# One pass over 512-token chunks for the feed-forward block and its backward, with token-major activations made by DMA transposes

## The chip, the cores and the metric

The kernel runs on one core of one Trainium2 chip. The metric is the device time of one execution in microseconds (us). The engines are named as the profile names them: PE is TensorE (matrix products), DVE is VectorE, ACT is ScalarE, POOL is GpSimd, and SP is SyncE, which issues most DMAs. "PEclk" is the TensorE clock that was granted, as a share of full speed.

## The reference, cut to what matters

A transformer block with modulated layer norms, forward, and then the gradients of all its nine inputs. There are 2048 tokens, D = 512, 32 heads of 16, and F = 1792 hidden features. All is bf16.

```python
h = layernorm(x) * (1 + ca) + sa
x = x + ga * (attention(h @ wqkv) @ wo)
h = layernorm(x) * (1 + cb) + sb          # xn2 is the normalised x, h2 this h
r = relu(h @ w1 + b1);  s = r * r
x = x + gb * (s @ w2 + b2)
# ... then jax.vjp of all this with grad_out
```

The backward of the feed-forward needs the same two large activations in two layouts. With `gf = gb * grad_out`, `ds = gf @ w2.T` and `dz = 2 * r * ds`, the input gradient `dz @ w1.T` wants s and dz *feature-major* (features on the 128 partitions), as does `s @ w2`. The weight gradients `dw1 = h2.T @ dz` and `dw2 = s.T @ gf` contract over tokens, so they want s and dz *token-major*. Each of the two tensors is 2048 x 1792 x 2 bytes, or 7.3 MB. One chunk of 512 tokens has 14 x 4 = 56 blocks of 128 x 128, that is 56 x 32 KB = 1.835 MB.

## The kernel before

The kernel before gets the second layout by computing the product a second time. The phases run one after another over all 2048 tokens, with DRAM in between. P is 128, DC is 4 (blocks of D), FC is 14 (blocks of F), QC is 4 (chunks of 512 tokens), TT is 16 (tiles of 128 tokens).

```python
# dense stage 1, feed-forward (cut)
for qc in range(QC):
    for fc in range(FC):                       # z, feature-major
        for ic in range(DC):
            PE.matmul(pz[:], w1_nat[:, ic, fc*P:(fc+1)*P], h2T[:, ic, qc*512:(qc+1)*512], ...)
        DVE.tensor_scalar(rT[:, fc, :], pz[:], b1col[:, fc:fc+1], 0.0, ALU.add, ALU.max)
    SP.dma_start(out=rT_st[qc], in_=...rT)     # to DRAM, for the backward
    DVE.tensor_tensor(sT[:], rT[:], rT[:], ALU.mult)
    for qi in range(4):
        t = qc*4 + qi
        for (f0, W) in fchunks:                # z AGAIN, token-major
            for ic in range(DC):
                PE.matmul(pzt[:, 0:W], h2T[:, ic, t*P:(t+1)*P], w1_nat[:, ic, f0:f0+W], ...)
            PE.matmul(pzt[:, 0:W], ones_bf[0:1, 0:P], b1row[0:1, f0:f0+W], ...)
            DVE.tensor_single_scalar(rtok[:, f0:f0+W], pzt[:, 0:W], 0.0, ALU.max)
        SP.dma_start(out=rtok_st[:, t, :], in_=rtok[:])
        DVE.tensor_tensor(stok[:], rtok[:], rtok[:], ALU.mult)
        SP.dma_start(out=stok_st[:, t, :], in_=stok[:])
        ...                                    # s @ w2, output
# weights for the backward (cut): w1T, w2T, gfT by DMA transposes, then
for t3 in range(3):
    for hg in range(HG):
        ...                                    # tmpT <- 128 columns of wqkv, transposed
        for hq in range(4):                    # 96 copies of 16 partitions x 1 KB
            SP.dma_start(out=wT_pad[o0:o0+DH, ..., :], in_=tmpT[r0:r0+DH, :])
# dense stage 2: ds, dzT, dz @ w1.T, backward of LN2 (cut)
# dense stage 3 (cut): ds AGAIN, token-major, 256 matmuls
#     DVE: dztok = 2 * ds * rtok (rtok reloaded), stored to dztok_st
# dw1: for each of 4 blocks of D, reload all of dztok (POOL and SP in turn)
# dw2: for each of 2 halves of F, reload all of stok
# then da, dO = da @ wo.T, dwo
# tail, after the backward of attention: dqkv, dh1 = dqkv @ wT_pad, backward of LN1
```

## Time and profile before

The time is 3955.47 us (median of 4 runs, 3953.62 to 3963.21). The table of windows gives, for each stretch of the span, its length and the busy time of each engine. It is the best first view here, because each stage has another limit and the page's shares average over them.

In the view below the columns are: window, its length, then PE, PEld (weight loads), DVE, ACT and POOL busy in us (with instruction counts), PEclk, the mean share of the 16 DMA engines that was busy, and GB/s. These are the windows of the kernel before, from attention forward to attention backward.

```profile
284.00:1223.00 939.00, 867.80 (x4102) 162.44 (x4101) 33.23 (x55) 938.90 (x1025) 19.14 (x31) 0.50 0.05 12
1223.00:1305.00 82.00, 32.95 (x195) 18.13 (x198) 67.53 (x234) 4.46 (x17) 0.61 (x1) 0.65 0.37 130
1305.00:1494.00 189.00, 184.07 (x784) 71.11 (x799) 140.42 (x192) 0.00 (x0) 0.00 (x0) 0.99 0.32 125
1494.00:1618.00 124.00, 11.81 (x27) 3.30 (x29) 10.11 (x24) 0.00 (x0) 6.93 (x1) 0.52 0.40 92
1618.00:1731.00 113.00, 110.99 (x468) 43.92 (x477) 93.05 (x326) 0.00 (x0) 0.00 (x0) 0.97 0.19 67
1731.00:1814.00 83.00, 54.45 (x244) 25.43 (x247) 44.26 (x88) 0.00 (x0) 1.29 (x2) 0.86 0.81 220
1814.00:1990.00 176.00, 103.04 (x251) 34.53 (x256) 11.94 (x30) 7.40 (x16) 17.16 (x32) 0.51 0.62 179
1990.00:2100.00 110.00, 57.47 (x219) 20.50 (x225) 3.12 (x3) 7.15 (x13) 15.28 (x24) 0.90 0.60 181
2100.00:2216.00 116.00, 68.95 (x335) 30.38 (x339) 53.47 (x127) 2.77 (x5) 48.22 (x58) 0.78 0.38 130
2216.00:3660.00 1444.00, 1237.81 (x10221) 343.94 (x10220) 1188.47 (x1024) 1118.68 (x2208) 139.78 (x102) 0.85 1.15 202
```

Row by row these are: attention forward; output projection and LN2; feed-forward forward; weights for the backward; backward product; second dz product; dw1; dw2; dO and dwo; attention backward. Attention forward is ScalarE without a gap (938.90 of 939). Attention backward is busy on PE, VectorE and ScalarE, and the change leaves its instructions as they are. What the change is meant to shorten is the 993 us between: PE is busy for 624 of them and no engine is full. The feed-forward row is PE-bound (184 of 189, clock 0.99); the row after it has 11.81 us of PE in 124 us.

Two views show what these rows hold. First the second products, as groups of the dense stages (line, engine, operation, names, shapes, count, busy us, mean ns of one, idle before): `pzt` is z again (product and its bias row), `pzg` is ds again. Together they are 60.0 + 22.9 + 56.6 = 139.5 us of PE, on top of the copies out of PSUM.

```profile
L433 PE MATMUL pzt<-w_nat,xn2T 128*128 128x512 bf16 (+1 forms) x252 | 60.0, 355 | 0.2
L566 PE MATMUL pzg<-w2T,gfT 128*128 128x512 bf16 (+1 forms) x251 | 56.6, 376 | 25.8 <-DVE dztok L568 25.4 <-issue 0.2
...
L435 PE MATMUL pzt<-b1row,ones_bf 1*128 1x512 bf16 x64 | 22.9, 358 | 0.0
```

Second, the queue of SyncE in the empty row (start, duration, name, count): groups of 16 small copies into `wT_pad` take 10 us each, about 0.63 us apiece, for 75 us in all with the transposes between. The loads for the next stage (`rTb` and `xn2b`) stand behind them, and VectorE waits 79.7 us for the first of these.

```profile
1535.31 10.30 SPq L487 DMA_DIRECT2D wT_pad<-tmpT  x16
...
1611.61 0.35 SPq L510 DMA_DIRECT2D rTb<-rT_st  x1
1612.02 0.89 SPq L528 DMA_DIRECT2D xn2b<-xn_st  x2
```

And the wait of VectorE in the dense stages (who waited, for whom: total us, times, longest). The view names `xn2b`, but the instruction at L518 reads `rTb` and not `xn2b`; the load of `rTb` is the one just ahead of it on the same queue:

```profile
DVE dzT L518 <- DMA xn2b<-xn_st: 79.7, 1, 79.7
```

### The profile page before, as it was taken

The numbers are of one execution on the slowest core, as the hardware profiler recorded it, in microseconds if no ns is written. First come the engines' busy times: TensorE is split into PE (matmuls) and PEld (weight loads), VectorE is DVE, ScalarE is ACT, GpSimd is POOL, SyncE is SP. The second block draws the span as 40 slices with busy tenths as digits, with TensorE's granted clock in tenths as the row PEclk, the third lists the DMA queues.
The fourth block names the chain that finished last, engine by engine and source line by source line (L and its number), as shares of the span: only waits on it lengthen the run. The fifth ranks groups of instructions, "written<-read, shape, count | busy, mean of one in ns | idle before, by whom it ended". The sixth has DMA issues, their size and how long they took to land. (4 is left out here: it accounts for less than half of the span.)

```text
span 3961.6 us, 49677 instructions
## 1 busy us (share of the span) xinstructions
PE 3084.2 (78%) x18427; PEld 898.6 (23%) x18501; DVE 2005.1 (51%) x3136; ACT 2143.6 (54%) x3486; POOL 279.7 (7%) x306
## 2 busy tenths in 40 slices
PE   3689999999996891676655788988888888888656
PEld 1231111111112330232222222222222222222212
DVE  7750000000006771563005587878878787887581
ACT  0019999999993000000000577877777787877211
POOL 2000000000000000000014110101010110101000
PEclk7885555555556895786587788879888887998877
DMA  3130000000002234246654799999999999999213
GB/s 120 63 123 5 15 17 16 17 16 15 6 5 97 111 132 94 99 113 207 180 171 148 157 198 209 203 203 208 203 210 197 212 198 209 196 200 197 105 49 102
DMA packets 1230145, 497.83 MB, mean 126 GB/s; under 512 B 1162051, under 2 KB 1192263, under 8 KB 1228109
## 3 DMA queue, kind: packets, MB, share of 16 engines
q1 hardware_dynamic: 1207246, 464.23, 55.2%
q0 software_dynamic: 6144, 28.32, 2.4%
q10 hardware_dynamic: 16512, 2.10, 0.4%
q8 instruction: 146, 2.39, 0.2%
q14 instruction: 97, 0.79, 0.1%
HBM read 126.45 MB, written 82.47 MB: 53 GB/s over the span
## 5 line engine op out<-in xcount | busy, mean ns | idle before, releaser
L754 DVE TENSOR_TENSOR dS_u<-psD_u,E_u 128x1024 bf16<-128x1024 f32 x1024 | 1188.5, 1216 | 297.2 <-PE psD_u L752 216.8
L742 ACT ACTIVATE E_u<-psS_u 128x512 bf16<-128x512 f32 x1536 | 868.8, 636 | 290.5 <-PE psD_u L752 276.1
L311 ACT ACTIVATE ET<-psST 128x1024 bf16<-128x1024 f32 x1024 | 938.8, 1770 | 0.0
L308 PE MATMUL psST<-qt_sb,kt_sb 32*128 32x512 bf16 x2048 | 622.7, 597 | 79.7 <-DMA kt_sb<-KtP 8.8
L740 PE MATMUL psS_u<-ik,iq 32*128 32x512 bf16 x1536 | 515.1, 429 | 14.1 <-ACT E_u L742 7.3
L326 DVE COPY ostage<-oacc 128x512 f32<-128x512 f32 x32 | 22.1, 692 | 914.3 <-PE oacc L322 828.4
L752 PE MATMUL psD_u<-iv,ido 32*128 32x512 bf16 x2048 | 444.3, 428 | 22.5 <-DVE dS_u L754 16.3
L792 PE MATMUL dqacc<-dsT,KS_tok 128*32 128x512 bf16 x2048 | 212.2, 501 | 161.2 <-DMA dsT<-dS_u 133.3
L742 ACT ACTIVATE E_u<-psS_x 128x512 bf16<-128x512 f32 x512 | 334.9, 654 | 3.7 <-PE psD_u L752 1.9
L322 PE MATMUL oacc<-ET,vaug 128*32 128x512 bf16 x2048 | 316.6, 608 | 0.6 <-ACT ET L311 0.6
L595 ACT ACTIVATE w1blk<-aw_0_12805 128x512 bf16<-128x512 f32 x1 | 0.6, 597 | 556.6 <-PE aw_0_12805 L591 556.6
L308 PEld LDWEIGHTS <-kt_sb 32*128 32x128 bf16 x2048 | 105.3, 99 | 557.6 <-issue 557.6
L777 PE MATMUL accVK<-E_u,dOs_tok 128*16 128x512 bf16 x2048 | 225.3, 430 | 0.0
L740 PE MATMUL psS_x<-ik,iq 32*128 32x512 bf16 x512 | 207.5, 405 | 1.0
L740 PEld LDWEIGHTS <-iq 32*128 32x128 bf16 x2048 | 100.1, 92 | 358.2 <-issue 357.5
L752 PEld LDWEIGHTS <-ido 32*128 32x128 bf16 x2048 | 124.7, 92 | 239.4 <-issue 218.0
L807 POOL TENSOR_TENSOR dQacc<-dQacc,dqtmp 128x512 f32<-128x512 f32 x64 | 81.1, 1268 | 849.9 <-ACT dqtmp L802 849.9
L515 PE MATMUL pds<-gfT,w2T 128*128 128x512 bf16 x219 | 55.2, 404 | 108.3 <-DVE dzT L518 79.0
L768 PE MATMUL accVK<-dS_u,qz_14371 128*32 128x512 bf16 x1024 | 112.0, 427 | 6.1 <-ACT vkb L780 6.1
L768 PE MATMUL accVK<-dS_u,qz_14372 128*32 128x512 bf16 x1024 | 111.5, 424 | 6.2 <-ACT vkb L780 5.9
L264 PE MATMUL ppad<-xn1T,wpadT 128*128 128x512 bf16 x376 | 97.0, 402 | 21.7 <-DVE stagep L267 16.2
L322 PEld LDWEIGHTS <-vaug 128*32 128x32 bf16 x2048 | 56.9, 101 | 224.1 <-issue 224.1
(1253 smaller groups left out, 2864.4 us busy)
## 6 DMA issues: line engine op xcount, KB each, us to landing
dzld<-dztok_st POOLq DMA_DIRECT2D x32, 448.0 KB, 3.7
dzld<-dztok_st SPq DMA_DIRECT2D x32, 448.0 KB, 3.4
dsT<-dS_u SPq DMA_TRANSPOSE x512, 4.8
rT_st<-rT SPq DMA_DIRECT2D x4, 1792.0 KB
rtok_st<-rtok SPq DMA_DIRECT2D x16, 448.0 KB, 2.5
stok_st<-stok SPq DMA_DIRECT2D x16, 448.0 KB
rTb<-rT_st SPq DMA_DIRECT2D x4, 1792.0 KB
rtokb<-rtok_st SPq DMA_DIRECT2D x16, 448.0 KB, 11.4
```

Source lines behind the costliest of these rows:

```text
L264: PE.matmul(pp[:], wpadT[:, ic, which, hg, :], h1T[:, ic, qc * 512:(qc + 1) * 512], start=(ic == 0), stop=(ic == DC - 1))
L308: PE.matmul(ps[:, hi, :], kt_sb[r:r + 32, kt * P:(kt + 1) * P], qt_sb[r:r + 32, qc * 512:(qc + 1) * 512], start=True, stop=True, tile_posi ...
L311: ACT.activation(ET[:, 2 * pair:2 * pair + 2, :], ps[:], AF.Exp, scale=SCALE)
L322: PE.matmul(oacc[32 * hq:32 * hq + 32, :], lhsT, ET[:, hq, :], start=(kt == 0), stop=(kt == TT - 1), tile_position=(0, 32 * hq), skip_grou ...
L740: PE.matmul(psS[:], st["q"][r:r + 32, qt * P:(qt + 1) * P], st["k"][r:r + 32, kc * 512:kc * 512 + 512], start=True, stop=True, tile_positi ...
L742: ACT.activation(bst[u][0][:, hq, :], psS[:], AF.Exp, scale=SCALE)
L752: PE.matmul(psD[:, hi, :], st["do"][r:r + 32, qt * P:(qt + 1) * P], st["v"][r:r + 32, kc * 512:kc * 512 + 512], start=True, stop=True, til ...
L754: DVE.tensor_tensor(dS_u[:, 2 * pair:2 * pair + 2, :], psD[:], E_u[:, 2 * pair:2 * pair + 2, :], ALU.mult)
L768: PE.matmul(cur["vk"][32 * hq:32 * hq + 32, :], hst[hg]["qz"][:, qt, hq, :], bst[u][1][:, hq, :], start=(qt == 0), stop=False, tile_positi ...
L777: PE.matmul(acc[32 * hq:32 * hq + DH, :], dOs_tok[:, qt, (hg * 4 + hq) * DH:(hg * 4 + hq + 1) * DH], E_u[:, hq, :], start=False, stop=(qt ...
L792: PE.matmul(acc[32 * hq:32 * hq + 32, :], KS_tok[:, kc * 4 + kt, h * DH:h * DH + 32], tT[:, :, hq * 4 + kt, :], start=(kt == 0), stop=(kt ...
L807: POOL.tensor_tensor(dst2, dst, tmp[:], ALU.add)
```

## The change

The intent: keep a chunk of 512 tokens on the chip from the output projection through the feed-forward, its backward and dO, and get the token-major s and dz by DMA transposes of the feature-major tiles. That removes the second products, most stores and reloads between the phases, and the stage that waits for weights: the padded transposed projection weight is built by POOL's own DMA queue under attention forward and kept in DRAM until the tail. The weight gradients then become one stage that loads each operand once. Attention forward runs by query chunk instead of by head group. Some elementwise work also moves: half of the relus go to ScalarE, h2 and the output's sum to POOL, and LN2's sums become one instruction. The first lines of the diff below remove; cuts are marked.

```diff
-                for (f0, W) in fchunks:
-                    ...PE.matmul(pzt[:, 0:W], h2T[:, ic, t*P:(t+1)*P], w1_nat[:, ic, f0:f0+W], ...)
-                    DVE.tensor_single_scalar(rtok[:, f0:f0+W], pzt[:, 0:W], 0.0, ALU.max)
-                SP.dma_start(out=rtok_st[:, t, :], in_=rtok[:])
-                ...                                # stok, second dz stage, rT store and reload
+        def dense_chunk(c):                        # called for c = 0..3, one after another
+            SP.dma_start(out=O_c[:], in_=o_st[:, ts, :]);  ...x0_c, g_c
+            SP.dma_start(out=OT..., in_=flat(O_c), transpose=True)
+            ...                                    # gf, gfT (transpose), a = O @ wo, x1, LN2 -> xn2_c
+            SP.dma_start(out=xn2T..., in_=flat(xn2_c), transpose=True)
+            ...                                    # h2T = xn2T * (1 + cb) + sb
+            for fc in range(FC):
+                ...PE.matmul(pz, w1_nat, h2T)      # rT on ACT and DVE in turn, sT = rT * rT on DVE
+            SP.dma_start(out=s_tok[:], in_=flat(sT), transpose=True)      # 56 blocks
+            SP.dma_start(out=stok_st[c], in_=flat(s_tok))
+            ...                                    # f = sT.T @ w2, output
+            for fc in range(FC):
+                ...PE.matmul(pds, w2T, gfT)        # dzT = 2 * ds * rT
+            SP.dma_start(out=dz_tok[:], in_=flat(dzT), transpose=True)    # 56 blocks
+            SP.dma_start(out=dztok_st[c], in_=flat(dz_tok))
+            ...                                    # dz @ w1.T, backward of LN2 -> dx1_c, da_c
+            SP.dma_start(out=daT..., in_=flat(da_c), transpose=True)
+            ...                                    # dO = da @ wo.T, dOT (transpose), to dOtP
-                    SP.dma_start(out=wT_pad[...], in_=tmpT[r0:r0 + DH, :])     # after feed-forward
+                    POOL.dma_start(out=wT_bld[...], in_=tmpT[r0:r0 + DH, :])   # under attention forward
+        POOL.dma_start(out=wT_st[:], in_=wT_bld[:])
+        # one weight-gradient stage: gf, O, da, h2 and all of s and dz loaded once,
+        # 4 + 14 + 4 output blocks of dwo, dw2, dw1
+    SP.dma_start(out=wT_pad[:], in_=wT_st[:])       # first load of the tail, 2 MB
-funits = [(hg, qc, kt) ...]                         # attention forward
+funits = [(qc, hg, kt) ...]
```

## The prediction

> **What bounds the kernel now.** Read as stages from the table of windows: projections 0-284 us; attention forward 284-1223 (ScalarE busy 938.9 of 939: saturated, PE clock 0.50); dense middle 1223-2216; attention backward 2216-3660 (DVE 1188, PE 1238 of 1444, DMA share 1.15); tail 3660-3962. The change acts on the dense middle, 993 us, where no engine is full: PE busy is 624 of 993.
>
> Inside it: output projection and LN2 82 us (PE 33); MLP forward 189 (PE 184, clock 0.99, so PE-bound); weight transposes 124 (PE 12; the DMA queue's timeline shows 96 wT_pad issues of 0.62 us, and behind them DVE waits 79.7 us); backward product 113 (PE 111); second dz product 83; dW1 176 (PE 103, clock 0.51, starved by dzld loads); dW2 110 (PE 57); dO, dwo 116.
>
> **Removed.** The 256+64 matmuls of the token-major s product and the 256 of the second dz (0.23 us each: 480 took 111 us in the backward product): about 125 us of PE. The 124 us stage: wT_pad is built during attention forward, where DMA share is 0.05; w1T, w2T and woT remain (w1T issue 1.26 us each). Four reloads of dz and two of s (44 MB) become one.
>
> **Added.** Per chunk 208 blocks of 128x128 through DMA transposes. The backward attention moves 16 blocks in about 2.8 us under load, landing in 4.8, so 36 us of DMA per chunk; s and dz (56 blocks, estimate 10-12 us each) hide under 13 us of matmuls; O, xn2, dA, dO do not hide.
>
> **The new critical path.** The instruction order runs chunks one after another. Per chunk, estimated from the durations: z 15, f 13, ds 12, dh 19 (VectorE, about 3.5 us per tile), dA transpose 6, dO 9, O load and transpose 10, projection and LN 15, xn2 transpose 5, h2 1: about 104 us, PE idle for some 40 of it. The skill's "TensorE: Matmul & The Clock Gate", Part 1, has 216 ns per warm 512-column matmul and half speed after an idle window; the trace agrees (clock 0.99 in the MLP, 0.53 in LN2).
>
> Chunk 0 waits for weights (queued ahead of its xn2 transpose), about 45 us after attention; four chunks then end about 435 us after attention. The weight-gradient stage reloads 22.7 MB (early loads ran near 330 GB/s: 7 MB in 21 us) against 544 matmuls (118 us): about 155-165 us, the first 21-30 exposed. Dense middle: about 615-640 us instead of 993.
>
> **Elsewhere.** Projections start about 10 us sooner (x before g). Attention forward may stall 0-30 us near its third head load: seven tmpT transposes precede it in the DMA queue, each waiting on eight POOL copies. Attention backward unchanged (same instructions). Tail +8 us (wT_pad, 2 MB, loaded ahead of the first tiles).
>
> **Predicted: 3600 us, range 3530 to 3680; faster 0.96, same 0.03, slower 0.01.**
>
> **What would show it.** No pzt or pzg groups; dense middle near 630 us in four repeats of about 104, PE busy about 60%; waits on xn2, dA and O transposes of about 5 us or more in each chunk; dW stage 150-170 with PE idle at its start on loads; attention forward within 940-970; backward 1440-1450.
>
> **What would make it wrong.** Large transposes far slower than 10-12 us (then dz waits on s's buffer, which sT, dzT and dOp share: +10-20 per chunk); attention forward blocked longer by POOL's copies; PE clock at half in the gappy chunks (+30 per chunk); gradient loads near 200 GB/s (+25).

## The result, and the profile after

The changed kernel takes 3624.12 us (median of 4 runs, 3619.38 to 3629.43) against 3955.47 us. The ratio is 0.916, with a 95% interval of 0.914 to 0.918. A ratio here is the mean time of one kernel's fast runs over the mean of the other's fast runs of the same rounds, so it is not quite the ratio of the medians that are quoted. The time is 24 us above the predicted 3600 and inside the range of 3530 to 3680.

The windows after, with the same columns. The rows are: attention forward; the gap until the first feed-forward product; chunks 0, 1, 2; chunk 3 with the wait for the gradients' loads; weight gradients with the first loads of attention backward.

```profile
290.00:1236.00 946.00, 869.25 (x4102) 163.53 (x4101) 33.42 (x56) 939.11 (x1025) 61.83 (x120) 0.50 0.11 33
1236.00:1301.00 65.00, 6.09 (x19) 2.66 (x21) 12.83 (x32) 3.88 (x6) 8.70 (x3) 0.55 0.81 200
1301.00:1408.00 107.00, 68.57 (x272) 26.48 (x275) 62.20 (x145) 7.41 (x12) 21.37 (x25) 0.79 0.60 150
1408.00:1517.00 109.00, 68.84 (x272) 26.59 (x276) 62.55 (x145) 7.40 (x12) 22.01 (x26) 0.80 0.58 145
1517.00:1626.00 109.00, 69.01 (x271) 26.71 (x276) 62.64 (x145) 7.40 (x12) 21.83 (x26) 0.80 0.59 140
1626.00:1744.00 118.00, 63.43 (x255) 24.84 (x261) 53.19 (x126) 4.81 (x7) 14.21 (x24) 0.76 0.67 161
1744.00:1874.00 130.00, 114.26 (x546) 53.92 (x555) 12.68 (x18) 13.06 (x22) 3.55 (x2) 0.93 0.51 198
```

The dense middle, 993 us before, is now 1236 to 1874, that is 638 us. On the spans of the two profiles (3961.6 and 3621.8 us) the balance is: from attention forward's last product to the first dS of attention backward 997.4 to 639.2 (-358), and elsewhere +18: attention forward starts 6 us later and lasts 6 us longer, the tail (from the last dS, which is VectorE's product in attention backward) is some 9 us longer, and attention backward is some 3 us shorter. A chunk takes 107 to 109 us, of which PE is busy for 69, at a clock of 0.79 to 0.80. So the chunk is a chain, not a wall of product, as predicted. These are PE's waits in chunk 1 (who waited, for whom: total us, times, longest):

```profile
PE pm L441 <- DMA T_10570<-O_m: 16.6, 1, 16.6
PE pm L472 <- DVE h2T L460: 13.7, 1, 13.7
PE prow L407 <- DVE proda L542: 5.4, 2, 2.7
PE pm L557 <- DMA T_10501<-da_c: 4.1, 1, 4.1
```

The transposes of O and dA, LN2 with the transpose of xn2 (the wait for h2T) and LN2's backward (the wait for `proda`) are the gaps: 4.1 + 16.6 + 13.7 + 5.4 us. The transposes of s and dz do not appear among the waits. The wait for O holds dO's transpose too: before chunk 3, dO's issues at 1596.27 us and takes 5.92, and O's comes behind it on the queue, at 1602.29.

Three spots cost more than predicted. At the front of chunk 0, PE waits for the first weights and then for h2T, whose transpose of xn2 stands on the queue behind 37 us of weight transposes. PE's timeline (start, duration, engine, line, operation, names, shapes, count; in brackets the idle time before it and what ended it):

```profile
1256.83 0.59 PE L441 MATMUL pm<-wo_nat,T_9372 128*128 128x512 bf16 x1 [15.03 <-DMA wo_nat<-in_A_wo_dram]
...
1301.53 8.69 PE L472 MATMUL pm<-h2T,w_nat 128*128 128x512 bf16 x32 [39.31 <-DVE h2T L460]
```

SyncE's timeline of the same stretch: w2T, w1T, woT, and only then xn2.

```profile
1259.17 13.69 SPq L399 DMA_TRANSPOSE w2T<-in_B_w_dram  x4
1272.90 18.51 SPq L401 DMA_TRANSPOSE w1T<-in_B_w_dram  x14
1291.46 5.17 SPq L403 DMA_TRANSPOSE woT<-in_A_wo_dram  x4
1296.74 1.93 SPq L457 DMA_TRANSPOSE T_9439<-xn_c  x1
```

In the last chunk the transpose of dA takes four times as long to issue as in the others. This is the view of its line (shortest, median and longest duration in ns, first and last start), chunk 2 first, then chunk 3:

```profile
L547 SPq DMA_TRANSPOSE T_11100<-da_c x1: 3113/3113/3113, 1580.3 to 1580.3; - x1
L547 SPq DMA_TRANSPOSE T_11699<-da_c x1: 12062/12062/12062, 1689.4 to 1689.4; - x1
```

The one thing that comes ahead of it only in chunk 3 is the store of db1. SyncE's timeline:

```profile
1678.81 0.58 SPq L586 DMA_DIRECT2D out_dram<-db1bf  x1
```

At the very start, VectorE casts 512 numbers for 17.69 us. VectorE's timeline, first of the kernel before:

```profile
15.18 4.54 DVE L117 CAST crows<-cbf 1x512 f32<-1x512 bf16 x1 [13.75 <-DMA cbf<-in_c_dram]
```

The same cast in the changed kernel, where its input comes earlier but its end, at 19.7 us, is the same:

```profile
2.02 17.69 DVE L112 CAST crows<-cbf 1x512 f32<-1x512 bf16 x1 [0.60 <-DMA cbf<-in_c_dram]
```

### The profile page after: what moved, and what is told of

The parts are those of the page before. It is cut to its first block, busy times and chain, and to the rows that moved or that the text cites. A ratio compares the mean times of both kernels' runs of the same rounds, so it can differ in the third digit from the quotient of the medians.

```text
span 3621.8 us, 47309 instructions
## 1 busy us (share of the span) xinstructions
PE 2861.2 (79%) x17554; PEld 811.5 (22%) x17605; DVE 1861.7 (51%) x2725; ACT 2166.0 (60%) x3501; POOL 338.4 (9%) x390
## 4 chain that ended last, share of the span: by engine, by line
PE 24%; DMA 17%; DVE 5%; ACT 5%; issue 3%; SPq 1%; POOL 0%; DVEq 0%; POOLq 0%; ACTq 0%
DMA dsT<-dS_u 14%; PE psS_u L686 6%; PE dqacc L738 4%; ACT E_u L688 4%; PE accVK L723 3%; PE accVK L714 2%; PE psS_x L686 2%; DVE dS_u L700 2%; PE aw L619 1%; SPq L910 1%; PE aw L628 1%; DVE dqkv_tok L814 1%; PE psD_u L698 1%; DVE dh1acc L822 1%; DMA iqs<-q_st 1%
## 5 line engine op out<-in xcount | busy, mean ns | idle before, releaser
L686 PE MATMUL psS_u<-ik,iq 32*128 32x512 bf16 x1536 | 523.3, 437 | 22.4 <-DMA ik<-KtP 13.4
L326 DVE COPY ostage<-oacc 128x512 f32<-128x512 f32 x32 | 22.1, 692 | 897.4 <-PE oacc L322 897.4
L442 ACT ACTIVATE a_c<-pm 128x512 bf16<-128x512 f32 x16 | 9.6, 597 | 260.7 <-PE pm L441 260.7
L472 PE MATMUL pm<-h2T,w_nat 128*128 128x512 bf16 x218 | 58.0, 432 | 81.0 <-DVE h2T L460 80.4
```

The lines of the kernel that those rows point to most:

```text
L686: PE.matmul(psS[:], st["q"][r:r + 32, qt * P:(qt + 1) * P], st["k"][r:r + 32, kc * 512:kc * 512 + 512], start=True, stop=True, tile_positi ...
```

## The experiments

There were twelve runs, all correct. Medians are set against the changed kernel's 3624.12 us. The kernel before was run again in each of the three batches of experiments (3960.29, 3953.85 and 3957.55 us, up to 6.4 us apart), so a difference under about 7 us between batches says nothing by itself; where it matters I give the ratio to the kernel before with its interval (0.9142 to 0.9177 for the changed kernel). The first batch was the slowest: by the ratios e_smm is +71, e_wsp +81 and e_dblT +38 us. "Pitch" below is the time from one chunk's first feed-forward product to the next chunk's.

| run | what | median us | against changed kernel | ratio to before |
|---|---|---|---|---|
| e_bT | before + transposes only | 3851.22 | (before - 109) | 0.9727 |
| e_smm | s by second product again | 3698.47 | +74.4 | 0.9338 |
| e_wsp | 96 copies back on SyncE | 3707.75 | +83.6 | 0.9364 |
| e_dblT | s and dz transposed twice | 3665.09 | +41.0 | 0.9256 |
| e_wearly | weights early | 3620.79 | -3.3 | 0.9155 |
| e_wmid | weights early, mended | 3592.86 | -31.3 | 0.9080 |
| e_pipe | next chunk's front moved up | 3552.90 | -71.2 | 0.8980 |
| e_dve | memsets off POOL | 3619.14 | -5.0 | 0.9150 |
| e_out5 | db1's store late | 3626.60 | +2.5 | 0.9167 |
| e_out5b | the same, mended | 3614.43 | -9.7 | 0.9135 |
| e_tail | order of the tail's loads | 3617.66 | -6.5 | 0.9141 |
| e_all2 | the good ones together | 3509.04 | -115.1 | 0.8867 |

### e_bT: the transposes alone, in the kernel before

```diff
-                rtok = ...; pzt product, relu, rtok store, stok = rtok * rtok, stok store
+            SP.dma_start(out=s_tok[:], in_=sT..., transpose=True)
+            SP.dma_start(out=stok_st[...], in_=s_tok...)
-    # dense stage 3: pzg product, dztok store
+            SP.dma_start(out=dz_tok[:], in_=dzT..., transpose=True)   # in dense stage 2
+            SP.dma_start(out=dztok_st[...], in_=dz_tok...)
```

> The kernel before with one part of the change alone: s and dz come token-major from DMA transposes of the feature-major tiles, the second product of each (52.9 us of h2 times w1T inside the first dense stage and the 83 us second-dz stage) is removed; stages, stores and reloads stay split, weight transposes stay. Theory (the split stages have a wall of PE product, so removing it shows): about 150 us sooner, 3780 to 3840 us. Rival (the gain of the whole change came from the fusion and from the fewer weight transposes, the second product alone hid in waits): less than 40 us sooner, 3915 us or more.

Measured: 3851.22 us, 109 us less than the kernel before in the same rounds. That is nearer the theory than the rival, but short of the 150 expected: of 139.5 us of PE removed, 78% came out as time. The trace tells where the rest stayed. The backward product gets going after its wait behind the `wT_pad` copies at 1560.8 instead of 1619.4 us: 58.6 us for the 83 us of product that left the feed-forward stage, where PE now waits 11.3 us for sT. And dw1 now begins with a wait of 25.0 us for VectorE's h2; in the kernel before, where the second dz product ran ahead of dw1, it is 3.7 us. That wait, 79.6 us here, is unchanged.

### e_smm: one second product put back into the changed kernel

```diff
-            SP.dma_start(out=s_tok[:], in_=flat(sT), transpose=True)
+            for ti in range(4):
+                for j in range(4):
+                    ...PE.matmul(pzt, h2T[:, ic, ti*P:(ti+1)*P], w1_nat[:, ic, 512*j:...]); bias row
+                    DVE.tensor_single_scalar(rt, pzt, 0.0, ALU.max); s_tok block = rt * rt
```

x is loaded into the tile of x1, to make room.

> The changed kernel with s token-major by a second product again (h2T against w1T, relu and square on VectorE), dz still by DMA transpose; wrong in nothing. It adds about 17 us of TensorE and about 16 x 1.05 us of VectorE work to each of the four chunks. Theory (a chunk of 107 to 109 us is a chain in which TensorE's products lie one after the other, so added product lengthens it): +60 to +110 us, 3685 to 3735 us. Rival (TensorE is idle for 40% of a chunk, so it absorbs the product): under +20 us.

Measured: +74.4 us, so 18.6 per chunk. The first products of chunks 0, 1 and 2 start at 1299.8, 1425.3 and 1551.2 us: a pitch of 125.5 to 125.9 us instead of 107 to 109 (PE's timeline, chunks 0 and 1):

```profile
1299.79 14.10 PE L473 MATMUL pm<-h2T,w_nat 128*128 128x512 bf16 x55 [38.97 <-DVE h2T L461]
...
1425.26 14.52 PE L473 MATMUL pm<-h2T,w_nat 128*128 128x512 bf16 x55 [13.89 <-DVE h2T L461]
```

PE is idle for over a third of a chunk, and the added 17 us lengthens the chunk all the same, because the idle time lies elsewhere in the chain. The rival falls.

### e_wsp: the 96 small copies back on SyncE, ahead of the chunks

```diff
-                    POOL.dma_start(out=wT_bld[...], in_=tmpT[...])   # under attention forward
+                    SP.dma_start(out=wT_bld[...], in_=tmpT[...])     # after attention forward
```

The whole build moves with the copies: the 12 tmpT transposes that feed them, POOL's memset and the store of the result.

> The changed kernel with the 96 copies that build the padded transposed projection weight issued by SyncE again, between attention forward and the first dense chunk, as in the kernel before (where SyncE issued them for 75 us). Theory (the move to the GpSimd queue under attention forward took those issues off the chain): +60 to +80 us, 3685 to 3705 us, and the three 5.9 us waits of ScalarE at the third head of attention forward vanish (-6 us of the same). Rival (the issues would be hidden behind the weights' load and the first chunk's products): within 15 us of the changed kernel.

Measured: +83.6 us. The theory holds, by a little more than its range. SyncE issues the copies from 1254 to 1328 (60 us for the 96 copies, 16 for the transposes, two of which come before 1254), and the first weight of the output projection comes only after them. SyncE's timeline, the last copies and that load:

```profile
1318.48 9.99 SPq L377 DMA_DIRECT2D wT_bld<-tmpT  x16
...
1336.30 0.39 SPq L389 DMA_DIRECT2D wo_nat<-in_A_wo_dram  x1
```

PE's timeline shows the wait that follows, against 15.03 us for the same product in the changed kernel:

```profile
1340.57 0.58 PE L442 MATMUL pm<-wo_nat,T 128*128 128x512 bf16 x1 [101.62 <-DMA wo_nat<-in_A_wo_dram]
```

The Trainium skill, "DMA: Bandwidth & Descriptors", section "Rules for kernel authors", says that spreading DMAs over several issuing engines brings no bandwidth and only saves the sequencer's issue time. No run here compares bandwidths. What this one shows is the other half: the issue of 1.5 MB in 96 copies of 16 KB takes 60 us of SyncE, and with its place on the queue the build is worth 84 us. The run changes the issuing engine and the moment together, so it does not say which of the two counts.

One part of the expectation failed. ScalarE's three waits of attention forward did not vanish. I had put them to the third head's load, behind the tmpT transposes; in this run there are no such transposes, and the waits are the same. ScalarE's timeline of the changed kernel shows where they are, every 256 exponentials (at 539.62, 776.37 and 1013.12 us, 1.98 us each), that is at the end of each 512-query chunk; the first is shown. There the transposes of the finished chunk's row sums (`prinv`) stand four in a row between the scores in PE's order, which this kernel sets by hand, and wait for VectorE's reciprocals (0.45 to 0.68 us each):

```profile
539.62 234.77 ACT L308 ACTIVATE ET<-psST 128x1024 bf16<-128x1024 f32 x256 [1.98 <-PE psST L306]
```

### e_dblT: the transposes of s and dz issued twice

```diff
             SP.dma_start(out=s_tok[:], in_=flat(sT), transpose=True)
+            SP.dma_start(out=s_tok[:], in_=flat(sT), transpose=True)
             ...
             SP.dma_start(out=dz_tok[:], in_=flat(dzT), transpose=True)
+            SP.dma_start(out=dz_tok[:], in_=flat(dzT), transpose=True)
```

> The changed kernel with the DMA transposes of s and of dz to token-major issued twice each (same result). Theory (they run under the products of the same chunk, and only the shared buffer and SyncE's order make others wait): 0 to +40 us, 3624 to 3664 us. Rival (the transposes are exposed in the chunk's chain): about 4 x 20 us, +80 us or more.

Measured: +41.0 us, at the edge of the theory's range and half of the rival's figure. The chunks' pitch is 117.9 to 120.2 us, so 10 to 11 more. In the waits of chunk 1 the one for dA's transpose grew from 4.1 to 12.5 us and a wait of 3.1 us for dzT appeared. So one transpose of s and one of dz are hidden. A second one of s costs those 3.1 us (dzT is written into the buffer that it reads), and a second one of dz is not hidden either: it holds SyncE for 8.47 us more and dA's transpose stands behind it. SyncE's timeline in chunk 1, the second transpose of dz and then dA's:

```profile
1477.72 8.47 SPq L512 DMA_TRANSPOSE dz_tok<-dzT  x1
...
1488.94 7.28 SPq L549 DMA_TRANSPOSE T<-da_c  x1
```

### e_wearly and e_wmid: weights loaded under attention forward

```diff
     wqkvpool.release()
+    ffw = tc.alloc_tile_pool(name="ffw", bufs=1)      # the weights get room of their own
+    # e_wearly: all loads and transposes right after the first head's load
+    # e_wmid: one by one at the ends of heads 4 to 19, each tied to the head's end:
+    #   DVE.tensor_copy(tile[0:1, ..., 0:1], ostage[0:1, 0:1]); SP.dma_start(out=tile, ...)
-        ...the same loads at the head of the dense phase
```

> The changed kernel with every weight and transposed weight of the dense chunks loaded before or during attention forward (they get room of their own then). Theory (the 65 us between attention forward and the first product of chunk 0 are mostly 7 MB of weights on the queue, with chunk 0's own transposes behind them): the first product of the feed-forward starts about 28 us after attention forward instead of 65, and the time falls by about 35 to 45 us, 3580 to 3590 us. Rival (chunk 0's front is as long by itself, from its O transpose, projection and LN2): under 10 us.

Measured: -3.3 us, ratio 0.9155 (0.9139 to 0.9172), which is no difference. But the mechanism was there. The first feed-forward product came 36.4 us after attention forward's last product (1289.0 after 1252.6) instead of 65.8 (1301.5 after 1235.7). More than half of that gain of 29.4 us had been lost already, at the start: attention forward ended 16.9 us later. The lead of 12.5 us that was left at the first feed-forward product shrank to 8.9 at the first weight gradient (chunk 0's pitch is 111.8 us instead of 107.2) and to 4.9 at the end of the trace. Attention forward began 6.3 us sooner (its first exponential at 283.71 instead of 290.04), but after the first head's 32 exponentials ScalarE waited 23.1 us for the second head's scores: the load of that head's queries came at 332.9 us, behind 39 us of weight transposes on SyncE's queue. ScalarE's timeline, the first head and the start of the second:

```profile
283.71 29.44 ACT L309 ACTIVATE ET<-psST 128x1024 bf16<-128x1024 f32 x32 [4.37 <-PE psST L307]
336.24 9.27 ACT L309 ACTIVATE ET<-psST 128x1024 bf16<-128x1024 f32 x10 [23.09 <-PE psST L307]
```

A load moved off one chain had been put on another. The mended version spreads the loads (its expectation speaks of 27 us and of the third head; the trace has 23 us at the second):

> The early loads mended: the changed kernel with the dense weights and transposed weights loaded one after another from the fourth to the nineteenth head of attention forward, each tied to that head's end by a copy of one element. Theory (the first early version won 29 us at the front of chunk 0 and lost 27 us because its transposes stood ahead of the third head's load on the queue): ScalarE's wait of 23.1 us is gone, attention forward ends at about 1236 as in the changed kernel, the first feed-forward product comes about 36 us after it instead of 66, and the time falls by 25 to 32 us. Rival (loads under attention forward slow its heads whenever they come): the time stays within 8 us of the changed kernel.

Measured: -31.3 us, ratio 0.9080 (0.9068 to 0.9092). The wait of 23.1 us is gone. Attention forward ends at 1227.4 and the first feed-forward product starts at 1265.0, so 37.6 us later. About 28 us of the gain are this. Another 8 come from attention forward's earlier end, because in this version the first `kt_sb` load happens to stand ahead of the tmpT transposes (it starts at 275.1 instead of 284.2 us); chunk 0 gives some of it back: its pitch is 113 us instead of 107, with a second wait for h2T of 3.5 us. PE's timeline, the first products of chunk 0:

```profile
1264.95 0.58 PE L480 MATMUL pm<-h2T,w_nat 128*128 128x512 bf16 x1 [10.01 <-DVE h2T L468]
1269.01 14.85 PE L480 MATMUL pm<-h2T,w_nat 128*128 128x512 bf16 x54 [3.47 <-DVE h2T L468]
```

### e_pipe: the next chunk's front inside this chunk

```diff
-        for c in range(QC):
-            for _ in dense_chunk(c): pass
+        next(gens[0])                       # O load, OT, projection, LN2, xn2T, h2T of chunk 0
+        for c in range(QC):
+            for _ in range(FC + 4): next(gens[c])       # z and f of chunk c
+            if c + 1 < QC: next(gens[c + 1])            # front of chunk c + 1
+            for _ in gens[c]: pass                      # ds, dh, dO of chunk c
```

O, a and xn2 get two buffers; x is loaded into the tile of x1, h2T is computed in place, and g's load, gf and its transpose come behind h2T instead of ahead of it.

> The changed kernel with the front of chunk c+1 (O's transpose, projection, LN2, xn2's transpose, h2T) written before the gradient half of chunk c, with two buffers for what crosses. Theory (a chunk of 108 us is 69 us of TensorE work with waits on the chain of transposes and LN2 between; another chunk's front fits in them): pitch of a chunk 108 to about 74 to 85 us, the time 60 to 110 us less, 3515 to 3565 us. Rival (the transposes collide on the one queue, or VectorE's 62 us per chunk with its waits sets the pitch): pitch stays over 98 us, under 30 us less.

Measured: -71.2 us, ratio 0.8980 (0.8966 to 0.8993). The pitch is 85 us, at the upper end of what was expected, and the three pitches account for the gain (22.1 + 24.0 + 24.3 us against the changed kernel's). The first products of chunks 0 and 1 in PE's timeline (those of 2 and 3 start at 1468.38 and 1553.12):

```profile
1298.33 14.74 PE L470 MATMUL pm<-T,w_nat 128*128 128x512 bf16 x56 [37.77 <-DVE T L451]
...
1383.46 12.25 PE L470 MATMUL pm<-T,w_nat 128*128 128x512 bf16 x56
```

The waits of 16.6 us for O and 13.7 us for h2T are gone from chunks 1 to 3. The last chunk has no successor to fill its gaps and takes 115 us to the first weight gradient (1668.0), and chunk 0's front is as exposed as it was.

### e_dve: the memsets at the start on VectorE

```diff
-    POOL.memset(vaug[:], 1.0);  POOL.memset(wpadT[:], 0.0)
+    DVE.memset(vaug[:], 1.0);   DVE.memset(wpadT[:], 0.0)
```

> The changed kernel with two memsets at the kernel's start (the padding of the augmented V and of the transposed projection weight) on VectorE instead of GpSimd. Theory (VectorE's cast of the small row constants took 17.69 us, against 2.02 before[...]): the cast takes under 3 us, the LN of the projections starts about 10 us sooner, the time 5 to 12 us less. Rival (the cast waits for its data, c or the modulation, from a DMA): the cast stays over 10 us, and the time within 3 us.

The theory was that POOL's memsets hold the cast. (Its "2.02 before" is a slip: the cast took 4.54 us in the kernel before, and 2.02 is its start in the changed kernel.) The cause of the long cast is settled; its worth is not what I thought. The cast now takes 0.35 us, with POOL's memsets gone (VectorE's timeline):

```profile
10.70 0.35 DVE L112 CAST crows<-cbf 1x512 f32<-1x512 bf16 x1
```

Since the cast starts late here, this run alone would not exclude that it waited for its data. The two kernels do: the cast ends at 19.7 us in both, whether it starts at 15.18 or at 2.02, and that is 0.3 us after the end of POOL's second memset. POOL's timeline in the kernel before (9.11 us in the changed kernel):

```profile
9.12 10.33 POOL L167 MEMSET wpadT<- 128x12288 bf16 x1
```

The Trainium skill, "SBUF — State Buffer", section "Who interferes with whom", has that a cast in a two-port mode and a GpSimd instruction exclude each other for the whole of the instruction. This run agrees: 17.69 us beside POOL's memsets, 0.35 without them (no view shows the cast's mode). The time, 3619.14 us with a ratio of 0.9150 (0.9134 to 0.9166), overlaps the changed kernel's interval. In the trace the LN starts at 33.6 instead of 37.0 us, and ScalarE's first exponential 1.6 us sooner (288.41 against 290.04). The memsets' 7.54 + 5.18 us now stand in VectorE's own chain. And x's load still waits: it starts at 29.6 us here, 33.1 us in the changed kernel and 4.7 us in the kernel before. In the changed kernel SyncE waits there for PE's last product of the preparation (`pcol`), so the x tile seems to take room that the preparation still holds. No run changes that place, so this reason is read from the waits and not tested.

### e_out5 and e_out5b: db1's store

```diff
         DVE.tensor_copy(db1bf[:], db1acc[:])
-        SP.dma_start(out=out_5.rearrange("(fc p) -> p fc", p=P), in_=db1bf[:])
+        # e_out5: the same line, written at the end of the weight-gradient stage
+        # e_out5b: behind the first of the four blocks of dw1, and made to depend on it:
+        #   DVE.tensor_copy(db1bf[0:1, 0:1], w1blk[0:1, 0:1]); DVE.tensor_copy(db1bf, db1acc); store
```

> The changed kernel with the store of db1, single 2-byte elements scattered over the partitions, moved from the last chunk to the end of the weight-gradient stage. Theory (this store sits on the queue ahead of the last chunk's transpose of dA, whose wait was 13.2 us against 4.1 us in the other chunks): that wait falls to 4 to 5 us, the time about 9 us less. Rival (the last chunk waits for another reason, such as LN2's backward, or the store costs the same later): within 3 us.

Measured: 3626.60 us, no difference, and the trace shows why this run tests nothing: SyncE issues the store at 1678.80 us, in the same place as before. The line was moved in the program, but the scheduler orders the queue, and the store waits for nothing later. (dA's transpose took 9.99 us to issue.)

> The test of db1's store mended: in the first version the compiled queue order was the same as before, so nothing was tested. Here the store depends on a block of the last weight gradient and so comes at the end of that stage. Theory (the scattered store delays the last chunk's transpose of dA: issue 12.06 us against 3.1 us in the other chunks): the transpose issues in about 3.1 us, TensorE's wait before the last dO product falls from 13.2 to 4 or 5 us, and the time falls by about 8 us. Rival (the last chunk's transpose is slow for another reason): wait stays over 10 us, time within 3 us.

Measured: 3614.43 us, -9.7, ratio 0.9135 (0.9123 to 0.9148), with five rounds. The interval just touches the changed kernel's, so the reading rests on the trace as well. The store now comes at 1808.97 us, dA's transpose issues in 3.17 us and PE waits 4.12 us instead of 13.24. SyncE's timeline of the last chunk:

```profile
1685.07 3.17 SPq L547 DMA_TRANSPOSE T<-da_c  x1
```

And PE's, at the product that needs it:

```profile
1690.10 5.11 PE L557 MATMUL pm<-woT,T 128*128 128x512 bf16 x16 [4.12 <-DMA T<-da_c]
```

So 3.5 KB in 1,792 elements of two bytes cost 9 us of the critical chain. The Trainium skill, "DMA: Bandwidth & Descriptors", section "Rules for kernel authors", has that a strided last dimension becomes one descriptor per element. The slow store has exactly that form. No view counts its descriptors, but in the changed kernel the DMA engines are partly busy (20 to 90%, in slices of about 1 us) from 1683 to 1694 us and move 55 GB/s or less; here they are idle between dz's store and the transpose.

### e_tail: the order of the tail's first loads

```diff
-        SP.dma_start(out=wT_pad[:], in_=wT_st[:])     # then x0, dx1, then the first inputs
+                if hg == 0: SP.dma_start(out=wT_pad[:], in_=wT_st[:])   # after the first inputs
+                if hg == 2: ...x0_tok, dx1_tok
```

> The changed kernel with the padded transposed weight (2 MB) loaded behind the first head group's inputs of the tail, and x and dx behind the third group's. Theory (the first product of the tail waits 24.75 us, 16.5 before the change, because 2 MB of weight and the inputs of the backward of LN1 stand ahead of its own inputs on the queue): that wait falls to 12 us or less and the time by 8 to 15 us. Rival (the product needs the weight anyway, so the order of the loads does not matter): within 4 us.

Measured: 3617.66 us, -6.5, ratio 0.9141 (0.9129 to 0.9154): between the two expectations, and the intervals overlap. The first wait fell as expected, from 24.75 to 8.51 us. PE's timeline, first of the changed kernel:

```profile
3339.95 0.26 PE L806 MATMUL ptq<-identb,xst_31231 128*128 128x128 bf16 x1 [24.75 <-DMA xst_31231<-dQtP]
```

Then of this run:

```profile
3322.16 0.37 PE L808 MATMUL ptq<-identb,xst 128*128 128x128 bf16 x2 [8.51 <-DMA xst<-dQtP]
```

But the transposes that now run early fill that time only in part. The product against the weight itself starts at 3330.7 us instead of 3340.0, and the next head group still waits for its inputs. Also SyncE's order was not the one I wrote: x and dx still went out right behind the weight, at 3319.7 and 3320.2 us. From attention backward's last product to the end of the span the tail is 4.7 us shorter.

### e_all2: together

The pipeline, the mended early weights, the tail's order, the late store; besides, the tmpT transposes and 96 copies are moved to heads 20 to 31 of attention forward.

> A candidate: the pipelined chunks, the mended early weights, the copies of the padded transposed projection weight moved from the start of attention forward to its heads 20 to 31, the tail's load order, and db1's store at the end of the weight gradients. If the gains add: 71 for the pipeline, about 28 for the weights, 6 for the three waits at the third head, 10 for the tail, 8 for the store, that is about 3500 us; if they overlap (the weights' wait and the pipeline share chunk 0's front, which stays exposed in both): 3500 to 3535. Above 3545 only the pipeline has counted.

Measured: 3509.04 us (3503.86 to 3513.81), ratio to the kernel before 0.8867 (0.8854 to 0.8880). It beats both kernels: 11.3% less than before, 3.2% less than the changed kernel. The single gains 71.2 + 31.3 + 9.7 + 6.5 = 118.7 us against 115.1 measured, so they add within the drift between batches. The "6 for the three waits" in the expectation was wrong for the reason that e_wsp showed: ScalarE still waits 1.98, 1.97 and 1.97 us at the ends of the chunks.

## Why the prediction was right or wrong

**Right: what bounds, and why the gain is large.** The dense middle was the place, and it went from 993 to 638 us (predicted 615 to 640, "near 630"). Two of the causes are shown by runs: the second products, worth 109 us by themselves in the kernel before (e_bT), and the small copies on SyncE's queue, worth 83.6 us (e_wsp). If the two add, the rest of the 331 us, about 138, no run isolates. The fusion, the single reload and the moved elementwise work are all in it, and the windows put it at the weight gradients: dw1 and dw2 took 176 + 110 us at clock 0.51 and 0.90 before, waiting for reloads; the one stage after, with dwo in it, takes 130 us at 0.93, behind a wait of 35 us. The trace of e_bT, which has the transposes without the fusion, sharpens this: its weight gradients take 343 us on PE's timeline (301 for dw1 and dw2, 42 for dwo) against 148 in the changed kernel, and the other work of its middle 537 us, with some 80 us of waiting behind the copies, against 473 for the four chunks. So apart from the copies the fused chunks are not shorter than the split stages; what is left of the gain lies in the weight gradients. That is a reading of two traces, not a test.

**Right in part by luck: the sum.** The prediction's own terms, 435 us for the chunks and 155 to 165 for the gradients, make 590 to 600, not "615-640". Measured were 473 for the chunks, 148 for the gradients and 17 until the first dS of attention backward, which no term names: 638. The chunks were too short in the prediction, the gradients too long, and the unnamed margin covered the difference.

**Right: the chunk is a chain.** "PE idle for some 40 of it": 107 to 109 us with 69 of PE. That s and dz "hide under 13 us of matmuls" and "O, xn2, dA, dO do not hide" is what the waits show, and e_dblT and e_smm confirm the first from two sides, e_pipe the second for O and xn2. The size was off by 3 to 5 us per chunk. In chunk 3 the terms measured 15.0 for z (15), 15.0 for f (13), 12.5 for ds (12) and 21.2 for dh (19); the last includes two waits of PE of 2.7 us for VectorE at its end.

**Mis-sized: chunk 0.** "Chunk 0 waits for weights ... about 45 us after attention": it was 65.8. The weights' transposes alone took 13.69 + 18.51 + 5.17 us of the queue, and the xn2 transpose stood behind them. e_wmid takes 28 us of it away.

**Missed: db1's store.** "Four chunks then end about 435 us after attention"; they ended at 1709, so 473. Of these 38 us, 21 are chunk 0's front, 13 the longer pitch of three chunks, and the rest, about 4, the last chunk. There a scattered store, unchanged from the kernel before, had come to stand ahead of a transpose that PE waits for (e_out5b: 9 us); the other parts of that chunk were shorter than predicted.

**Mis-sized the other way: weight gradients.** "About 155-165 us, the first 21-30 exposed": PE waited 35.2 us and then worked almost without a gap, about 148 us in all. The longer wait is no slow load: the loads issue 17 us after PE's last product, behind dO's transpose and stores, and then run at 326 to 435 GB/s. The shorter stage paid back part of chunk 0's excess.

**Wrong: "Projections start about 10 us sooner (x before g)".** They start 4 us later (LN at 37.0 instead of 33.1) and attention forward starts 6 us later (290.0 instead of 284.1). The cast of `crows` ends at the same time in both kernels, 19.7 us, because POOL's memsets hold it; x's load now starts at 33.1 us instead of 4.7; and 2.5 us of tmpT transposes stand ahead of the first `kt_sb` load. In e_wsp, where they do not, the first exponential comes 2.7 us sooner.

**Right in size, wrong in place: "Attention forward may stall 0-30 us near its third head load".** It lasts 6 us longer, but not there: three waits of 1.98 us at the ends of the query chunks. That the size fits is luck. The danger at a head's load was real all the same: e_wearly ran into it at the second head, for 23 us.

**Right: attention backward and the tail.** The backward has the same instructions and took some 3 us less; the tail is 9 us longer (predicted +8), with the first product waiting 24.75 us. What would have made the prediction wrong (slow transposes, PE at half clock, gradient loads near 200 GB/s) did not come. The Trainium skill's "TensorE: Matmul & The Clock Gate", Part 1, which the prediction used, has the clock fall after idle stretches, and this agrees: 0.79 to 0.80 in the gappy chunks, 0.93 in the weight gradients and 0.99 in the feed-forward stage before.

## What to carry to other kernels

A second product for a second layout is worth replacing by a DMA transpose when the transpose can run under other product of the same chunk; count then what else stands on the transposing queue, because a transpose holds it for microseconds. Many small copies cost their place on a queue more than their bytes, so issue them, and one-element scatters too, where nobody waits behind them. When a load is moved to an earlier stage, look at which load of that stage now stands behind it, and check in the trace that the move happened at all.

## What the Trainium skill lacked or had wrong

- "DMA: Bandwidth & Descriptors", "Latency and other measured facts", gives DMA transposes 261 GB/s with a non-contiguous middle dimension, and 350 to 400 when contiguous. Here a transpose of 56 blocks (1.835 MB, tile to tile) ran at a steady 200 to 222 GB/s in the profile's slices of 0.35 us (s in chunk 3) and took 8.4 us to issue: below both figures.
- I found no rule on the same page for how long a transpose holds the issuing engine as it grows; its table on trn3 has one sequencer time for earlier generations, in cycles for 8,192 tiles. Here it grew with the size: 1.8 to 4.4 us for 16 blocks, 4.9 to 6.1 for 32 (dO), 8.4 to 9.1 for 56, and later DMAs of the same queue waited behind it (e_dblT: PE's wait for dA's transpose grew by 8.4 us).
- The same page, "Rules for kernel authors", warns of one descriptor per element, but that row gives no cost. Here a store of 1,792 two-byte elements delayed the next transpose on the queue by 9 us (issue 12.06 us against 3.17 us).
